# Attention with a GEGLU feed-forward on one Trainium2 core: more seven-product pairs in the last blocks, with their steps in turns

## The chip, the core and the metric

The kernel runs on one NeuronCore of a Trainium2 chip. Times are device microseconds of that core; the time of a kernel is the median of several executions, and one execution is profiled. Five engines work in parallel, each through its own queue in order: PE (TensorE, matrix products into PSUM), ACT (ScalarE), DVE (VectorE), POOL (GpSimd) and SP (SyncE, which issues most DMAs). An engine waits for another through semaphores. PEld is TensorE's weight load, which overlaps its products.

## The reference

```python
def _attn_ref(q, k, v):                       # q, k, v: (8, 8, 576, 64) float32
    q_s = np.exp(q - max over d);  q_s = q_s / sum over d
    k_s = np.exp(k - max over s);  k_s = k_s / sum over s
    kv = einsum('bhsd,bhse->bhde', k_s, v)
    return einsum('bhsd,bhde->bhse', q_s, kv)

def _moe_ref(x, w_gate, w_val, w_out):        # x: 4608 tokens x 512
    g = x @ w_gate                            # 512 x 1536
    gelu = 0.5 * g * (1 + erf(g / sqrt(2)))
    val = x @ w_val                           # 512 x 1536
    return (gelu * val) @ w_out               # 1536 x 512
```

The heads of the attention output are laid side by side (8 heads x 64 = 512 columns) and go into the feed-forward part as x. Nearly all arithmetic is in the three products with the weights.

## The kernel before, in words

**Blocks.** The 4608 tokens are worked on in nine blocks of 512. Blocks 0 to 7 are the batches, of whose 576 tokens 512 each; block 8 is made of the 64 remaining tokens of every batch (`xtr`). The order is 0 to 6, then 8, then 7 (`order`, L507). A block has a gate stage (g and val for 12 slices of 128 columns of the inner width, the result in `ht`) and an output stage. The program is written out in the order of its instructions for every engine; `at(block, kind, place, ...)` (L844) hangs attention work and other side work into places of that order and `ride` (L926) emits it. So what is written first stands first in its engine's queue.

**Gate stage, blocks 3 and later** (`fi_pairs`, L583). A slice can be computed classically (`half`, L587: four matmuls of 512 tokens for g, four for val; ACT takes the Gelu of g into a tile of the tag `gl`, DVE multiplies into `ht`). Or two slices, k and k + 3, make a *pair* and are computed with seven products on quarters (Strassen's scheme in Winograd's form): `product_gv` (L572), each of four matmuls of 256 tokens, 28 for the pair where the classical way has 16 of 512. Three pairs (k = 0, 1, 2: slices 0 to 5) are done so, slices 6 to 11 classically. For the pairs the kernel needs sums of the weights (`sum_wgv`, L556, on DVE into `ws`, one sum in place in the weights) and of x (`sum_x`, L566, four on POOL into `xs`, which has one buffer).

A pair in four steps of the queue, with `half` calls between them:
1. product 1 into bank pa, copied by ACT into pb (L623); product 5 into pc, snapshot s5 by ACT (`snap`, L606);
2. product 6 added in pa, snapshot s2; product 3 added in pc; DVE writes `cc[:, 0]` (`add`, L611); pc is free;
3. product 7 added in pa, DVE writes `cc[:, 1]`; product 2 added in pb, `final` (L599: ACT Gelu `glq`, DVE product into `ht`); then the upper half: ACT's Gelu `glc` of `cc` (L639) and POOL's product into `ht` (L640);
4. product 4 added in pa, which DVE must have read for `cc[:, 1]`; `final`.

`gl`, `glq`, `glc` and the output stage's snapshots `sn` share the tag `gl` with four buffers in turn; `cc` has one buffer. Banks of PSUM go round in a ring (`big`, L80); `hold` keeps one until `let_go`.

**Output stage** (`out_strassen`, L668): seven products again, of twelve matmuls each (`product`, L651), in the order 1 (psa), 2 (psb), 5 (psc), 6 (psa), 3 (psc), 7 (psa), 4 (psa). It needs sums of `ht` (`sum_h`, L542) for 5, 6, 3 and 7; sums 1 and 2 of a group are on DVE, sums 3 and 4 on DVE or POOL. The groups j = 0 and 1 come in the gate stage after their pair (kind PR, L923), the last group at the output stage's start (L961). DVE snapshots psa and psc (L690) before the next product is added into them. In block 8 `late` is set (L707): product 2 stands after product 7, and one of the sums moves.

**Side work.** Per batch: Exp of q and k on ACT, sums and reciprocals of q's rows on DVE (`norm_sum`, L210, one for each pair of heads; `norm_pair`, L219, for two of them), products with them on POOL (`norm_mul`), a transposing DMA (`unit_td`, L359), the cast of v on POOL (`cast_v`, L201, 640 columns at a time), the product of k and v (`unit_kv4`, L312) and of q with that into x (`unit_x4`, L398, at place NS 4, between products 7 and 4 of the block before). The 64 remaining rows of batch 0 go their own way: loaded by two DMAs into `q0r` with batch 2 (L851), `exp_rem0` (L240) at the end of block 2, `norm_rem0` (L244) on DVE and a transposing DMA (`unit_trem`, L350) in block 3, multiplied in block 3's NS 4 (L914). Tiles for q rows after Exp (`eq`, two buffers) and for loaded k (`kt`, two buffers) take turns by batch.

Of the kernel before, what the change touches and what calls it, by code (L numbers as in the profile page):

```python
# [18 lines left out]
def kernel(  # L19
# [86 lines left out]
    for i in range(2):  # L106
# [6 lines left out]
    ws = {nm: const.tile([P, 3, 2, NO // 2 * P], f16, name=f"ws{nm}") for nm in "gv"}  # L113
    xs = const.tile([P, 4, 2, 256], f16)
    q0r = const.tile([64, H, D], f32)
    eq0r = const.tile([P, C], f16)
    ld_b = {nm: [const.tile([P, H, NC * D], f32, name=f"{nm}t{i}") for i in range(n)]
            for nm, n in (("k", 2), ("v", 1), ("q", 1))}

# [29 lines left out]
    def load(src, nm, b, h0, h1, n0):  # L149
        tiles[(nm, b)] = ld_b[nm][b % len(ld_b[nm])]  # L150
        for t, c0 in ((0, n0), (1, 1)):
            (nc.scalar if b == 0 and t == 1 else nc.sync).dma_start(
                out=tiles[(nm, b)][t:P:2, h0:h1, c0 * D:NC * D],
                in_=src[b, h0:h1].rearrange("h (m n) d -> m h (n d)", n=NT)[
                    :, :, (4 * t + c0) * D:(4 * t + NC) * D])
# [36 lines left out]
    def exp(nm, b, h0=0, h1=H, n0=0):  # L192
        dst = ek_b[0] if nm == "k" else eq_b[b % 2]
        o, i = (("p n (c t d) -> p c t n d", "p c t (n d) -> p c t n d") if b >= QUAD else
                ("p n (h d) -> p h n d", "p h (n d) -> p h n d"))
        nc.scalar.activation(  # L196
            out=dst[:, n0:NC, h0 * D:h1 * D].rearrange(o, d=D, **({"t": 2} if b >= QUAD else {})),
            in_=heads(tiles[(nm, b)], b, h0, h1)[..., n0 * D:NC * D].rearrange(i, d=D),
            func=ACTF.Exp)
# [10 lines left out]
    def norm_sum(b, hp, n0=0):  # L210
        n = NC - n0
        e = eq_b[b % 2][:, n0:NC, hp * P:(hp + 1) * P].rearrange("p n (h d) -> p n h d", d=D)
# [6 lines left out]
    def norm_pair(b, g, n0, engs):  # L219

        n = NC - n0
        e = eq_b[b % 2][:, n0:NC, 2 * g * P:(2 * g + 2) * P].rearrange("p n (h d) -> p n h d", d=D)
# [16 lines left out]

    def exp_rem0():  # L240
        nc.scalar.activation(out=eq0r[0:64, :].rearrange("p (h d) -> p h d", d=D), in_=q0r,
                             func=ACTF.Exp)

    def norm_rem0():  # L244
# [5 lines left out]
        nc.vector.tensor_tensor(  # L250
# [84 lines left out]
    def unit_t(b, g, eng="dve", between=()):  # L335
# [3 lines left out]
        for j in range(2):  # L339
            hp = 2 * g + j  # L340
            for f in between if j == 1 else ():
                f()
            for n in range(NM):
                nc.tensor.transpose(
                    pst[:, j, n * P:(n + 1) * P],
                    eq_b[b % 2][:, n + 1, hp * P:(hp + 1) * P], ident)
# [3 lines left out]
    def unit_trem(b):  # L350

        src = eq0r[0:64] if b == 0 else eq_b[b % 2][:, 0, :]
# [6 lines left out]
    def unit_td(b):  # L359
# [3 lines left out]
                                    in_=eq_b[b % 2].rearrange("p n c -> p (n c)"))  # L363
# [192 lines left out]
    def sum_wgv(nm, i):  # L556
        w = wg_sb if nm == "g" else wv_sb
        n = NO // 2 * P
        a11, a21 = w[:, 0:2, 0:n], w[:, 0:2, n:2 * n]
        a12, a22 = w[:, 2:4, 0:n], w[:, 2:4, n:2 * n]  # L560
        t = [ws[nm][:, i] for i in range(3)]
# [10 lines left out]
    def product_gv(i, ps, xt, k, first):  # L572
        lo, hi = slice(k * P, (k + 1) * P), slice((k + NO // 2) * P, (k + NO // 2 + 1) * P)
        for t, w, nm in ((0, wv_sb, "v"), (1, wg_sb, "g")):
            for c in range(2):
                a = {1: w[:, c, lo], 2: w[:, 2 + c, lo], 3: ws[nm][:, 2, c, lo], 4: w[:, 2 + c, hi],
                     5: ws[nm][:, 0, c, lo], 6: ws[nm][:, 1, c, lo], 7: w[:, c, hi]}[i]
# [5 lines left out]
    def fi_pairs(b, xt):  # L583
        cs = [(c, nm) for k in range(NO // 2) for c in (NO + k, NO + NO // 2 + k) for nm in "gv"]
        psg = {}

        def half(n):  # L587
            c, nm = cs[n]
            t = big([P, 512], f32, "ps" + nm)
            mm_gv(t, wg_sb if nm == "g" else wv_sb, xt, c, range(HP))  # L590
            if nm == "g":
                psg[c] = ffn.tile([P, 512], f32, name="gl", tag="gl")
                nc.scalar.activation(out=psg[c], in_=t, func=ACTF.Gelu)  # L593
            else:
                nc.vector.scalar_tensor_tensor(out=ht[:, c, :], in0=t, scalar=_H_SCALE,  # L595
                                               in1=psg[c], op0=ALU.mult, op1=ALU.mult)
            ride(b, HF, n)

        def final(ps, fi):  # L599
# [6 lines left out]
        def snap(ps):  # L606
            sn = ffn.tile([P, 2, 256], f32, name="snq", tag="snq", bufs=3)
# [6 lines left out]

        ride(b, HF, -1)
        half(0)
        half(1)
        for k in range(NO // 2):
            cc = ffn.tile([P, 2, 2, 256], f32, name="cc", tag="cc", bufs=1)
# [6 lines left out]
            s5 = snap(pc)  # L626
            half(3 * k + 2)
# [5 lines left out]
            half(3 * k + 3)  # L633
# [4 lines left out]
            glc = ffn.tile([P, 2, 256], f32, name="glc", tag="gl")  # L638
            nc.scalar.activation(out=glc, in_=cc[:, :, 1], func=ACTF.Gelu, scale=1.0 / _H_SCALE)  # L639
            nc.gpsimd.tensor_tensor(  # L640
                out=ht[:, k:NO:NO // 2, 256:512], in0=cc[:, :, 0], in1=glc, op=ALU.mult)
            half(3 * k + 4)
            product_gv(4, pa, xt, k, False)
            final(pa, k + NO // 2)
            if k == NO // 2 - 1:
                half(11)
            ride(b, PR, k)
# [3 lines left out]
    def product(i, ps, first, ts=(0, 1)):  # L651
        for j in range(NO):
            for t in ts:
# [5 lines left out]
                if w is None:  # L659
# [3 lines left out]
                                 stop=(j == NO - 1), skip_group_check=True)  # L663

# [3 lines left out]
    def out_strassen(b, last):  # L668
# [38 lines left out]
        late = b == B  # L707
        get("a")
        product(1, ps["a"], True)
        s1 = snap("a")  # L710
        if not late:
            second()
# [5 lines left out]
        s5 = snap("c")  # L718
        if late:
            sum_h(*last_js(b), (3,))  # L720
# [4 lines left out]
        add("c", s2, 0, 1)  # L725
        for x in tiles_["c"]:
            let_go(x)
# [7 lines left out]
        ride(b, NS, 4)  # L735
        if late:
# [104 lines left out]
    FI, NS, HF, PR = range(4)  # L841
# [7 lines left out]
    def load_2nd():  # L849
        load_batch(2, ((q, "q"), (k, "k")))  # L850
        for h0 in (0, 4):  # L851
            nc.sync.dma_start(out=q0r[:, h0:h0 + 4], in_=q[0, h0:h0 + 4].rearrange(
                "h (m n) d -> m h (n d)", n=NT)[:, :, 0:D])
# [42 lines left out]
    at(2, FI, NFI - 1, L(exp, "q", 4), L(exp, "k", 4), exp_rem0)  # L896
    at(3, HF, 8, L(norm_rem0))
    at(3, HF, 11, L(unit_trem, 0))
    for b in range(3, B):
        n = b + 1  # L900
        if n < B:
            at(b, HF, -1, L(norm_sum, n, 0), L(norm_mul, n, 0, "pool"), L(norm_sum, n, 1),
               L(norm_mul, n, 1, "pool"))
            at(b, HF, 1, L(norm_sum, n, 2), L(norm_mul, n, 2, "pool"))
            at(b, HF, 2, L(norm_sum, n, 3), L(norm_mul, n, 3, "pool"))
            at(b, HF, 3, L(unit_td, n))
        if n + 1 < B:
            at(b, HF, 0, L(load_2, n + 1))
            at(b, HF, 5, L(cast_v, n + 1, 0, 4))
            at(b, HF, 8, L(cast_v, n + 1, 4, 8))  # L910
            at(b, HF, 11, L(exp, "q", n + 1), L(exp, "k", n + 1))
    for b in range(2, B - 1):
        n = b + 1
        at(b, NS, 4, L(unit_x4, n, ("act", "dve"), 0 if n == 4 else None))  # L914
# [4 lines left out]
        at(b, NS, 4, L(preload, ACTF.Gelu), L(lambda n: sum_x(get_xt(n)), n) if n < B - 1 else L(sum_x, xtr))  # L919
    at(B, NS, 2, L(lambda: sum_x(get_xt(B - 1))))  # L920
    for b in range(3, B + 1):
        for j in range(NO // 2 - 1):
            at(b, PR, j, L(sum_h, j, NO, (1, 2)), L(sum_h, j, NO, (3, 4), "pool"))  # L923
# [6 lines left out]
    for b in order:  # L930
# [9 lines left out]
        if b > 2:  # L940
            fi_pairs(b, xt)
# [51 lines left out]
```

## Time and profile before

| what | us |
|---|---|
| median of 3 runs | 301.37 (301.36 to 301.57) |
| the profiled execution | 301.16 |
| its span, first to last instruction | 299.4 |
| block 3, gate stage from 113.87 | 21.6 |
| blocks 4, 5, 6, gate stages from 146.28, 176.73, 206.91 | 19.5 to 19.6 each |
| output stages of blocks 4 and 5 | 10.9, 10.6 |
| block 8, gate stage from 236.55, output stage from 256.08 | 19.5, 10.35 |
| block 7, gate stage from 266.43; output stage from 285.96 to the end | 19.5, 13.4 |

The page gives the busy time of each engine. A block can be found in PE's timeline by its first `psg` matmul after the `psa<-tw,ht` ones of the output stage. A matmul's own duration (0.27 us at 256 tokens, 0.38 at 512) is longer than the distance to the next one, since matmuls are pipelined; ACT and DVE instructions overlap their followers by about 0.1 us too. A timeline's columns are start, duration, engine, line, operation, output from inputs, shapes and count, and in brackets the idle time before and what ended it. The table of stretches gives, for a window, its length and each engine's busy time and instructions.

### The profile page before, as it was taken

To read this page: it belongs to the slowest core of one execution; us is meant where nothing else is said; L and a number is where in the kernel's file an instruction comes from. 1 tells how busy PE (TensorE), PEld (TensorE's weight loads), DVE (VectorE), ACT (ScalarE), POOL (GpSimd) and SP (SyncE) were. 2 spreads that over 40 slices of the span, in tenths; PEclk is the share of its full clock that TensorE was granted. 3 is DMA by queue.
4 is the path that set the end of the run, shared out by engine and by line. 5 is a ranking of instruction groups with operands and counts; after the bars stand their busy time and mean duration, and the time that the engine had idled before them with its cause. 6 is when DMAs were issued, how large, how long until landed. Compare 5 with 4: busy or idle time off the path is not lost. (4 is left out here: it accounts for less than half of the span.)

```text
span 299.4 us, 5905 instructions
## 1 busy us (share of the span) xinstructions
PE 287.1 (96%) x2293; PEld 188.4 (63%) x2293; DVE 213.5 (71%) x411; ACT 173.1 (58%) x269; POOL 161.7 (54%) x149
## 2 busy tenths in 40 slices
PE   3999999999999999899999999999999999899994
PEld 1544445446744586568666876687668666676683
DVE  2953479998767889786867786878687557845762
ACT  4763467777652576558656956595652465126530
POOL 1557558870336009991599359944981536803610
PEclk9999999999999999999999999999999999999999
DMA  7999999997189106960399029802140300023003
GB/s 225 372 383 390 400 389 388 332 319 208 74 286 306 42 2 227 384 100 2 127 344 233 3 113 347 242 2 101 54 77 0 123 21 0 2 61 81 0 2 140
DMA packets 54619, 51.69 MB, mean 173 GB/s; under 512 B 18496, under 2 KB 50496, under 8 KB 54592
## 3 DMA queue, kind: packets, MB, share of 16 engines
q1 hardware_dynamic: 52864, 49.49, 52.0%
q10 hardware_dynamic: 1728, 1.84, 1.9%
q8 instruction: 18, 0.29, 0.4%
q14 instruction: 9, 0.07, 0.1%
HBM read 37.75 MB, written 9.44 MB: 158 GB/s over the span
## 5 line engine op out<-in xcount | busy, mean ns | idle before, releaser
L443 PE MATMUL psg<-xt,wg_sb 128*128 128x512 f16 x264 | 69.8, 379 | 0.0
L443 PE MATMUL psv<-xt,wv_sb 128*128 128x512 f16 x264 | 69.7, 379 | 0.0
L443 PEld LDWEIGHTS <-wv_sb 128*128 128x128 f16 x288 | 28.1, 98 | 27.4 <-issue 0.2
L233 POOL TENSOR_TENSOR eq<-eq,rrq 128x640 f16<-128x640 f16 (+1 forms) x27 | 34.5, 1297 | 19.7 <-DVE rrq L226 7.3
L443 PEld LDWEIGHTS <-wg_sb 128*128 128x128 f16 x288 | 28.1, 98 | 25.3
L661 PEld LDWEIGHTS <-ht 128*128 128x128 f16 x384 | 37.2, 98 | 7.1 <-issue 0.8
L448 ACT ACTIVATE gl<-psg 128x512 f32<-128x512 f32 x36 | 21.0, 597 | 29.0 <-PE psg L443 28.9
L640 POOL TENSOR_TENSOR ht<-cc,glc 128x512 f16<-128x512 f32 x18 | 22.8, 1267 | 24.1 <-ACT glc L639 24.1
L449 DVE SCALAR_TENSOR_TENSOR ht<-psv,gl 128x512 f16<-128x512 f32 x36 | 24.2, 684 | 16.0 <-PE psv L443 13.7
L570 POOL TENSOR_TENSOR xs<-xt 128x512 f16<-128x512 f16 x10 | 12.0, 1200 | 43.1 <-ACT xt L174 43.1
L595 DVE SCALAR_TENSOR_TENSOR ht<-psv,gl 128x512 f16<-128x512 f32 x36 | 24.6, 684 | 4.5 <-PE psv L443 2.4
L593 ACT ACTIVATE gl<-psg 128x512 f32<-128x512 f32 x36 | 21.3, 591 | 7.9 <-PE psg L443 7.8
L172 POOL CAST v<-vt 128x640 f16<-128x640 f32 x26 | 19.1, 769 | 12.0 <-PE pskv L319 10.5
L661 PE MATMUL psa<-tw,ht 128*128 128x256 f16 x192 | 23.5, 273 | 0.2 <-DVE yo L696 0.2
L214 DVE TENSOR_REDUCE rq<-eq 128x10 f32<-128x640 f16 x28 | 22.2, 793 | 1.6 <-ACT eq L196 1.6
L196 ACT ACTIVATE ek<-kt 128x1280 f16<-128x1280 f32 (+1 forms) x11 | 19.1, 1748 | 5.6 <-DMA kt<-in_k_dram 4.1
L580 PEld LDWEIGHTS <-wv_sb 128*128 128x128 f16 x144 | 14.0, 98 | 12.8 <-DVE cc L612 1.8
L661 PEld LDWEIGHTS <-sh 128*128 128x128 f16 x192 | 18.7, 98 | 3.5 <-issue 1.0
L552 POOL TENSOR_TENSOR ht<-ht 128x512 f16<-128x512 f16 x12 | 16.7, 1396 | 6.5 <-DVE sh L552 6.5
L196 ACT ACTIVATE eq<-qt 128x2560 f16<-128x2560 f32 (+2 forms) x10 | 18.4, 1863 | 2.6 <-DMA qt<-in_q_dram 2.5
L601 ACT ACTIVATE glq<-pgb 128x256 f32<-128x256 f32 x18 | 6.9, 383 | 21.6 <-PE pgb L580 21.2
L612 DVE SCALAR_TENSOR_TENSOR cc<-pgc,snq 128x512 f32<-128x512 f32 x18 | 12.4, 686 | 7.5 <-ACT snq L608 7.5
(136 smaller groups left out, 566.5 us busy)
## 6 DMA issues: line engine op xcount, KB each, us to landing
out_dram<-yo SPq DMA_DIRECT2D x15, 512.0 KB, 3.4
kt<-in_k_dram SPq DMA_DIRECT2D x7, 640.0 KB, 8.4
vt<-in_v_dram SPq DMA_DIRECT2D x7, 640.0 KB, 5.1
qt<-in_q_dram SPq DMA_DIRECT2D x7, 640.0 KB, 6.8
qt<-in_q_dram SPq DMA_DIRECT2D x8, 512.0 KB, 7.4
wost<-in_moe_w_out_dram SPq DMA_DIRECT2D x6, 512.0 KB, 7.9
kt<-in_k_dram SPq DMA_DIRECT2D x6, 512.0 KB, 9.8
vt<-in_v_dram SPq DMA_DIRECT2D x6, 512.0 KB, 5.7
```

The source lines that it names most:

```text
L172: nc.gpsimd.tensor_copy(out=dst, in_=src)
L196: nc.scalar.activation(out=dst[:, n0:NC, h0 * D:h1 * D].rearrange(o, d=D, **({"t": 2} if b >= QUAD else {})), in_=heads(tiles[(nm, b)], b, ...
L214: nc.vector.reduce_sum(rq, e, axis=mybir.AxisListType.X)
L233: (nc.gpsimd if eng == "pool" else nc.vector).tensor_tensor(out=e, in0=e, in1=rrq.unsqueeze(-1).to_broadcast((P, n, 2, D)), op=ALU.mult)
L443: nc.tensor.matmul(ps, w[:, ci, fi * P:(fi + 1) * P], xt[:, ci, :], start=(ci == 0), stop=(ci == HP - 1))
L448: nc.scalar.activation(out=gl, in_=psg, func=ACTF.Gelu)
L449: nc.vector.scalar_tensor_tensor(out=ht[:, fi, :], in0=psv, scalar=_H_SCALE, in1=gl, op0=ALU.mult, op1=ALU.mult)
L552: (nc.gpsimd if eng == "pool" else nc.vector).tensor_tensor(out=o, in0=a, in1=b, op=op)
L593: nc.scalar.activation(out=psg[c], in_=t, func=ACTF.Gelu)
L595: nc.vector.scalar_tensor_tensor(out=ht[:, c, :], in0=t, scalar=_H_SCALE, in1=psg[c], op0=ALU.mult, op1=ALU.mult)
L640: nc.gpsimd.tensor_tensor(out=ht[:, k:NO:NO // 2, 256:512], in0=cc[:, :, 0], in1=glc, op=ALU.mult)
L661: nc.tensor.matmul(ps[t], a, w, start=(first and j == 0 and (t == ts[0] or ps[t].tensor is not ps[ts[0]].tensor)), stop=(j == NO - 1), ski ...
```

## The change

It touches the gate stages of blocks 3 to 8.

- **Pairs.** Blocks 4, 5 and 6 compute a fourth pair (k = 6: slices 6 and 9) with seven products, blocks 8 and 7 all six pairs (k = 0, 1, 2, 6, 7, 8) and no slice classically. Block 3 keeps three.
- **Order.** A string per block lists the steps: `k.i` is step i of pair k, `7g` and `7v` are the halves of a classical slice, letters are places for side work, `s0` and `s1` the sums of `ht`. In blocks 8 and 7, and in part of 4 to 6, the steps of two pairs take turns. The last step of the last pair (8.4) stands in the output stage after product 1, its upper half goes to DVE and is written after step 2.4, and the first step of block 7 stands in block 8's output stage before product 4.
- **Weight sums** for the new pairs are made on DVE at the places NS 1, 2 and 3 of the output stages of blocks 3 to 6, in the space of the second `kt` buffer. `cc` gets a second buffer in the space of the second `eq` buffer. So from batch 4 on k and q have one buffer each. `snq` has four buffers, not three.
- **Norm sums** from block 3 on are taken by two head pairs at once (`norm_pair`), both products on POOL.
- **Batch 0's remainder** is loaded in block 4, in two tiles, its Exp is at the end of block 4, its norm in block 5 (NS 2, product on POOL), its transposing DMA in block 6, its product in block 6's NS 4.
- Block 8's output stage has the common order (`late = False`). The preload of the Gelu table is left out in block 6's NS 4. Small sums of x: in block 6 for block 8.

```diff
+    def buf(bs, b):
+        return bs[b % len(bs) if b < 4 else 0]
...
-    def sum_wgv(nm, i):
+    def sum_wgv(nm, i, k=0, n=NO // 2):
...
-        nc.vector.tensor_tensor(
+        nc.gpsimd.tensor_tensor(
             out=e, in0=e, in1=rrq.unsqueeze(-1).to_broadcast((64, H, D)), op=ALU.mult)
...
+    THREE = ("a 6g l 6v n 0.1 9g 0.2 9v t 0.3 7g 0.4 s0 1.1 7v c 1.2 10g 1.3 10v 1.4 s1 2.1 8g d 2.2"
+             " 8v 2.3 11g 2.4 11v e")
+    FOUR = ("a 7g l 7v n 0.1 10g 0.2 10v t 0.3 6.1 0.4 8g 6.2 8v c 6.3 1.1 6.4 s0 2.1 1.2 2.2 d 1.3"
+            " 2.3 11g 1.4 s1 2.4 11v e")
+    SIX = ("0.1 6.1 0.2 6.2 0.3 6.3 0.4 1.1 6.4 s0 7.1 1.2 7.2 1.3 7.3 1.4 2.1 7.4 s1 8.1 2.2 8.2"
+           " 2.3 8.3 2.4")
+    steps = {b: (THREE if b == 3 else SIX if b >= B - 1 else FOUR).split() for b in range(3, B + 1)}
...
+        def upper(cc):
+            glc = ffn.tile([P, 2, 256], f32, name="glc", tag="gl")
+            nc.scalar.activation(out=glc, in_=cc[:, :, 1], func=ACTF.Gelu, scale=1.0 / _H_SCALE)
+            (nc.vector if k == NFI - NO // 2 - 1 else nc.gpsimd).tensor_tensor(
+                out=ht[:, k:k + NO // 2 + 1:NO // 2, 256:512], in0=cc[:, :, 0], in1=glc, op=ALU.mult)
+
+        if i == 1:
+            live["odd"] = odd = not live.get("odd", True)
+            cc = cc_b if odd else ffn.tile([P, 2, 2, 256], f32, name="cc", tag="cc", bufs=1)
...
+            if k == NFI - NO // 2 - 1:
+                live["upper"] = lambda: upper(cc)
+            else:
+                upper(cc)
...
-        late = b == B
+        late = False
         get("a")
         product(1, ps["a"], True)
         s1 = snap("a")
+        if b >= B - 1:
+            pair_step(b, get_x(b), NFI - NO // 2 - 1, 4)
         if not late:
             second()
...
         s5 = snap("c")
+        ride(b, NS, 1)
...
         add("c", s2, 0, 1)
+        ride(b, NS, 3)
...
         ride(b, NS, 4)
+        if b == B:
+            go_on(B - 1, get_x(B - 1), 1)
...
+            at(b, PR, "a", L(norm_pair, n, 0, 0, ("pool", "pool")))
+            at(b, PR, "n", L(norm_pair, n, 1, 0, ("pool", "pool")))
+            at(b, PR, "t", L(unit_td, n))
         if n + 1 < B:
+            at(b, PR, "l", L(load_2, n + 1))
+            at(b, PR, "c", L(cast_v, n + 1, 0, 4))
+            at(b, PR, "d", L(cast_v, n + 1, 4, 8))
+            at(b, PR, "e", L(exp, "q", n + 1), L(exp, "k", n + 1))
+    at(4, PR, "l", load_rem0)
+    at(4, PR, "e", exp_rem0)
+    at(5, NS, 2, norm_rem0)
+    at(6, PR, "t", L(unit_trem, 0))
...
     for b in range(3, B + 1):
         for j in range(NO // 2 - 1):
-            at(b, PR, j, L(sum_h, j, NO, (1, 2)), L(sum_h, j, NO, (3, 4), "pool"))
+            at(b, PR, f"s{j}", L(sum_h, j, NO, (1, 2)), L(sum_h, j, NO, (3, 4), "pool"))
+    for b, i, what in ((3, 1, "g1 v1"), (3, 2, "g2 v2 g3 v3"), (3, 3, "g4 v4")):
+        for x in what.split():
+            at(b, NS, i, L(sum_wgv, x[0], int(x[1]), NO, 1))
+    for b, i, what in ((4, 1, "g1"), (4, 2, "g2 g4"), (4, 3, "v1"), (5, 1, "v2"), (5, 3, "v4"),
+                       (6, 1, "g3"), (6, 2, "v3")):
+        for x in what.split():
+            at(b, NS, i, L(sum_wgv, x[0], int(x[1]), NO + 1, 2))
```

## The prediction

> **What bounds the kernel now.** I read part 1 of the page first, then the table of stretches, cut at the first matmul of each block's gate stage, then PE's waits, and last the timelines of the engines around those waits.
>
> ```profile
> PE 287.1 (96%) x2293; PEld 188.4 (63%) x2293; DVE 213.5 (71%) x411; ACT 173.1 (58%) x269; POOL 161.7 (54%) x149
> ...
> core 0: us, PE busy (x) PEld busy (x) DVE busy (x) ACT busy (x) POOL busy (x), PEclk, DMA share, GB/s
> 146.28:165.85 19.57, 19.57 (x135) 12.90 (x132) 14.37 (x30) 13.01 (x27) 18.41 (x18) 1.00 0.86 242
> 206.91:226.44 19.53, 19.53 (x135) 12.92 (x132) 14.57 (x30) 12.94 (x27) 16.68 (x15) 1.00 0.25 61
> 236.55:256.08 19.53, 19.53 (x134) 12.91 (x132) 11.07 (x22) 12.55 (x25) 11.45 (x10) 1.00 0.07 29
> ...
> PE pga L580 <- DVE cc L612: 1.8, 2, 1.4
> PE psa L661 <- DVE sn L690: 0.8, 1, 0.8
> ```
>
> TensorE is never idle in the gate stages of blocks 4 (first stretch), 6 and 8, at granted clock 1.00, so a column less is time less. But POOL is busy for 18.41 us of block 4's 19.57; the average of 54% hides that. PE's waits are few: two in block 3 (product 4 waits for `cc`) and one in block 8's output stage.
>
> ```profile
> 256.50 1.15 POOL L570 TENSOR_TENSOR xs<-xt 128x512 f16<-128x512 f16 x1
> 257.73 1.22 POOL L570 TENSOR_TENSOR xs<-xt,xs 128x512 f16<-128x512 f16 x1
> 258.91 1.33 POOL L570 TENSOR_TENSOR xs<-xt 128x512 f16<-128x512 f16 x1
> ...
> 257.11 0.82 DVE L552 TENSOR_TENSOR sh<-ht 128x512 f16<-128x512 f16 x1
> 257.97 1.26 DVE L552 TENSOR_TENSOR sh<-sh,ht 128x512 f16<-128x512 f16 x1
> 259.15 0.68 DVE L690 TENSOR_SCALAR sn<-psa 128x512 f32<-128x512 f32 x1
> ...
> 259.88 1.47 PE L661 MATMUL psa<-tw,sh 128*128 128x256 f16 x12 [0.84 <-DVE sn L690]
> ```
>
> This is block 8's end; the last line is product 6. The DVE sums `sh` take 0.42 us alone; here 0.82 and 1.26, and each ends 0.28 us after the POOL instruction during which it began (257.65 and 258.95). The same holds at 65.66 (0.82) and 93.52 (0.84 where 0.55 is usual) beside a POOL cast. So **a DVE sum of two SBUF tensors waits for the running POOL instruction**; evacuations from PSUM (0.68) don't.
>
> **Gains.** Matmuls start 0.2163 us apart at 512 columns and 0.1092 at 256 (starts in the timeline of block 8). A classical pair is 16 x 0.2163 = 3.46; a seven-product pair 28 x 0.1092 = 3.06; 0.403 less. Nine pairs change (one each in blocks 4, 5, 6, three each in 8 and 7): **-3.63**. The weight loads, 98 ns each, still fit under 109. Block 8's wait above cost 1.17 with the gap inside the product before; the new order of that stage removes it: **-1.17**. Block 3: product 4 is 1.52 late at 122.33 behind four norm sums (115.76 to 120.42, 4.08 without the evacuation between), and 0.58 at 134.21 behind `norm_rem0` (1.57 of DVE). The reduce takes 0.793 at 640 elements and 1.216 at 1024, so 1.50 at 1280 (between 1.22 and 1.59); with reciprocals two pairs take 3.42, so 0.61 less, and the second wait goes: **-1.19**. Block 4's 0.24 at 171.32 goes with its new order. Sum **-6.2**.
>
> **Losses in blocks 4 to 6.** I lay the new order out from the block's first matmul (0), with starts back to back as the timelines of block 8 show: ACT 0.49 to 0.50 for 512, 0.27 for 256, 0.54 for `glc`; DVE 0.61, 0.34, and sums 0.46 + 0.35; POOL product 1.27, sums 1.39 + 1.15, cast 0.69; hand-over about 0.05. The four pairs and eight halves take PE 19.15. POOL ends the norm products at 8.6 as before (154.92 - 146.28), then: product of pair 0 to 9.8, casts "c" to 11.2, product of pair 6 from 12.3 to 13.6 (its `glc` waits for step 6.3). At s0 DVE's sums wait for the final of 6.4: P4 ends at 12.3, ACT first has the copy and snapshot of 1.1, so the Gelu starts at 13.15 and DVE is done at 14.0. POOL's two sums then run to 17.1, casts "d" to 18.4, products of pairs 1 and 2 to 19.7 and 20.9. POOL has 18.41 + 1.27 = 19.7 us of work for 19.15: it is the engine that becomes late.
>
> Who waits: the tag `gl` has four buffers; step 1.4's Gelu gets the one that `glc` of pair 1 holds until POOL's product at 19.7. So its final ends at 20.5. Behind it on DVE stand the sums of s1, the first of which begins during POOL's product of pair 2 and ends 0.28 after it, 21.2; the second 21.6; only then comes the final of step 2.4, at 22.0. Output product 1 reads that row (ht 5) with its last two matmuls, due 1.09 after its start at 19.15 + 0.27 (0.27 are short waits in the steps, by the same laying): 20.5. **1.5 late.** Next: POOL's s1 sums run 21.3 to 23.8; DVE's last sums begin at 22.6, are held to 24.1 and 24.5; the snapshot ends at 25.1, the one of psc at 27.15. Products 5, 6 and 3 wait 0.1, 0.2 and 0.7: **1.0**. Blocks 4 and 5: 0.27 + 2.54 each. Block 6 has no casts: 0.27 + 0.83 + 1.02. Sum **+7.7**.
>
> **Losses in blocks 8 and 7.** Per pair ACT needs 3 x 0.495 + 0.54 + 2 x 0.27 = 2.57, DVE 2 x 0.61 + 2 x 0.345 + 0.4 = 2.3, POOL 2.5, all under PE's 3.06; but the order in the queues costs: copy of pair 7 stands behind the Gelu of 6.4, and `cc` of 1.3 behind it in turn: 0.16 + 0.06 + 0.06 + 0.18 per two pairs, twice: 0.95 a block. In the end stage, from the start of product 1: the final of 2.4 is done at 1.28, which costs 0.24; POOL's product of pair 2 ends at 1.53; DVE's `upper` of pair 8 runs 1.3 to 2.0 (a row bounds it: 0.42 to 0.69, taken 0.69); the last sums begin at 2.05. In block 8 POOL runs `sum_x` from 1.5: the sums are held to 3.0 and 4.3, the snapshot ends at 4.9, and only then the final of 8.4, at 5.25. Product 2 needs its row at 3.08: **2.2 late**. In block 7 POOL is idle: final at 3.6, 0.59 late. Sum 2 x 0.95 + 2 x 0.24 + 2.2 + 0.6 + 0.1 = **+5.3**.
>
> [...]
>
> **Edits costed at nothing, with their cover.** The weight sums at NS 1 to 3 are DVE work of 1.9 (block 3: eight of 256 columns), 1.5, 0.7 and 0.7 us; 512 columns take 0.42 (`sh`), 256 I take as 0.29 by the step 0.42 to 0.55 of 512 to 768, bounds 0.2 and 0.42. They lie behind snapshots where DVE idles (0.53, 0.62, 0.62 in block 5's output stage; 8.37 busy of 10.88 in block 4's). Without that cover up to 4.8. `norm_rem0` in block 5: 0.9 of DVE in the same idle time; its POOL product (1.48 for a like one of 128 rows) when POOL is idle. Two small DMAs of q go from batch 2's loads to behind batch 6's on SP's queue, before a transposing DMA that waited for POOL until 185.20 anyway (loads issued by 183.6); the transposing DMA of the remainder goes to block 6, used 12 us later. `exp_rem0` as two instructions: 0.76 of ACT before a wait of 2.5. One k and one eq buffer from batch 4 on: loads of k issue 6 us after the Exp that frees them, Exp of q starts 4.7 after the transposing DMA landed.
>
> **Sum.** -6.2 + 7.7 + 5.3 = **+6.7** (rounded). The profiled execution took 301.16 (span 299.4 and 1.8 around it), 0.2 under the median of 301.37: 301.2 + 6.7 = **307.9**. Laid in the same way, the old order ends within 0.2 us of the profile, so the forecast rests on the new order's waits.
>
> **Rivals.** (1) *TensorE stays the bound, faster.* The output-stage losses (5.1 + 1.85 + 2.5 + 0.8 = 10.2) all hang on DVE standing in front of finals and snapshots for POOL's last product. If that lands some 2.3 us earlier than I say (by 18.6 in blocks 4 to 6), they go, and 297.7 results. For: PE never idles in the old stages, DVE and ACT have a third to spare. Against: 18.41 of 19.57 on POOL, and one product added. (2) *Slower by less.* The hold of DVE by POOL applies only beside `sum_x`-like pairs or is rarer than laid: the queue order remains (about 1.4 in each of blocks 4 and 5, 0.7 in 6, 1.1 and 0.6 in the last two, 0.27 to 0.95 inside). These sum to 7.9 and give 302.9. For: in blocks 4 to 7 now every sum takes 0.42. Against: there they never meet POOL; where they do (four places) they are held. (3) *The waits cancel the gain:* POOL about 1.5 us earlier in blocks 4 to 6 alone takes 7 us off: 300.9.
>
> **Chances.** Forecast (304.5 to 310.7) 0.62; rival 2 (302 to 304.5) 0.18; above 310.7, as when the weight sums lose half their cover and the step waits double, 0.03; no change 0.05 (within 0.2%, 0.6 us, about what a measurement can tell); rival 1 0.12. Faster 0.12, same 0.05, slower 0.83. The range reaches from 302.0 to 310.7 and leaves out 0.2.
>
> **What would show it.** Right: PE waits in product 1 of blocks 4 and 5 for `ht` from DVE (L602 of before), about 1.5 each; psc waiting for a snapshot by 0.7; `sh` sums above 0.8 us in blocks 4 to 6 and 8; POOL's product of pair 2 ending over 1 us into the output stage; product 2 of block 8 late by 2. Wrong: POOL done before the output stage, or sums of 0.42 beside POOL work. PE busy should fall by some 3.6.

## The result and the profile after

The changed kernel takes **309.82 us** in the median of four executions (308.1, 309.65, 310.0, 310.04), the kernel before 301.42 (301.36 to 301.57): a ratio of 1.027, with a 95% interval of 1.023 to 1.030. The forecast was 307.9 in a range of 302.0 to 310.7. The profiled execution of the changed kernel took 310.0, its span is 308.1.

The first part of the page after the change, and the table of stretches for the gate stages of blocks 4 and 6 (columns as in the prediction's table; each window ends some 0.1 before its stage does):

```profile
PE 290.5 (94%) x2401; PEld 198.8 (65%) x2401; DVE 225.8 (73%) x430; ACT 186.2 (60%) x305; POOL 171.5 (56%) x157
...
core 0: us, PE busy (x) PEld busy (x) DVE busy (x) ACT busy (x) POOL busy (x), PEclk, DMA share, GB/s
145.12:164.50 19.38, 19.32 (x146) 14.07 (x144) 13.51 (x24) 13.62 (x29) 17.14 (x17) 1.00 0.87 252
210.09:229.40 19.31, 19.27 (x146) 14.04 (x144) 13.69 (x24) 13.85 (x30) 14.99 (x14) 1.00 0.27 66
```

PE is nowhere really idle inside the gate stages, and they are hardly shorter than before: by the starts in PE's timeline blocks 4 to 6 take 19.46 to 19.49 (19.53 to 19.57 before), block 8 takes 19.01 (19.53). What the page gives as busy rose by 3.4 us although the pairs save PE work. Part of that is a stretch at half clock, shown below; part are short waits, which lie within the modelled ends of the matmuls and count as busy. So the share in part 1 tells little here; the waits tell more. PE's waits after the change, without the first row (4.9 us at the kernel's start, as before) and the last (0.3, for `kv_sb`):

```profile
PE psb L706 <- DVE ht L629: 3.0, 2, 2.4
PE psa L706 <- DVE ht L629: 2.7, 3, 1.0
PE psc L706 <- DVE sn L738: 1.7, 3, 0.6
PE pga L601 <- DVE cc L639: 0.6, 1, 0.6
```

All four name DVE, none POOL. The first is product 2 of blocks 8 and 7, the second product 1 of blocks 4 to 6, the third product 3 of the same blocks, which waits for the snapshot of psc; the last is product 4 of block 3. The length of a block, from its first gate matmul to the next block's, shows where the time went (starts in PE's timelines; "side work alone" is the run e4 below, which has none of the new pairs):

| kernel | block 3 | 4 | 5 | 6 | block 8's start to PE's last matmul |
|---|---|---|---|---|---|
| before | 32.41 | 30.45 | 30.18 | 29.64 | 58.76 |
| after | 30.97 | 32.50 | 32.47 | 31.41 | 62.85 |
| side work alone | 30.96 | 30.18 | 30.18 | 29.64 | 58.76 |

Block 3 gained 1.44, blocks 4 to 6 lost 6.1, blocks 8 and 7 lost 4.1.

**Blocks 4 to 6.** The end of block 4's gate stage: timelines of POOL, DVE and PE.

```profile
163.39 1.28 POOL L645 TENSOR_TENSOR ht<-eq,glc 128x512 f16<-128x512 f32 x1
164.62 1.28 POOL L645 TENSOR_TENSOR ht<-cc,glc 128x512 f16<-128x512 f32 x1
...
165.46 0.71 DVE L572 TENSOR_TENSOR sh<-ht 128x512 f16<-128x512 f16 x1
166.21 0.42 DVE L572 TENSOR_TENSOR sh<-sh,ht 128x512 f16<-128x512 f16 x1
166.55 0.42 DVE L629 SCALAR_TENSOR_TENSOR ht<-pga,glq 128x256 f16<-128x256 f32 x1
...
167.03 0.39 PE L706 MATMUL psa<-wo_sb,ht 128*128 128x256 f16 x2 [1.03 <-DVE ht L629]
```

POOL's products for the upper halves of pairs 1 and 2 end at 164.67 and 165.90, the second some 1.3 us after the gate stage is over on PE. DVE's first sum of s1 is held by this second product (0.71 in place of 0.42) and ends 0.27 after it; the second sum follows; only then comes the final of step 2.4, for which the last two matmuls of product 1 wait.

That POOL's last product lands so late is not new. The same place before the change, one row each of POOL, DVE and PE:

```profile
166.08 1.27 POOL L640 TENSOR_TENSOR ht<-cc,glc 128x512 f16<-128x512 f32 x1
167.38 0.43 DVE L552 TENSOR_TENSOR sh<-ht 128x512 f16<-128x512 f16 x1 [0.44 <-POOL ht L640]
165.85 1.47 PE L661 MATMUL psa<-wo_sb,ht 128*128 128x256 f16 x12
```

It ended 1.50 after the gate stage (21.07 after the block's start, now 20.77), and product 1 ran through, since the finals stood ahead of the sums that waited for it. What did move is POOL's product before it, pair 1's: it ended 15.47 after the block's start and ends 19.55 now. For this one step 1.4's Gelu waits (for the buffer, as predicted), and behind its final come the sums of s1, which stand ahead of the final of 2.4.

**Block 8.** Its output stage on POOL (the sums of x), DVE and PE:

```profile
262.06 1.60 POOL L589 TENSOR_TENSOR xs<-xt 128x512 f16<-128x512 f16 x1
263.74 1.21 POOL L589 TENSOR_TENSOR xs<-xt,xs 128x512 f16<-128x512 f16 x1
264.91 1.33 POOL L589 TENSOR_TENSOR xs<-xt 128x512 f16<-128x512 f16 x1
...
261.84 0.81 DVE L645 TENSOR_TENSOR ht<-cc,glc 128x512 f16<-128x512 f32 x1
262.75 1.19 DVE L572 TENSOR_TENSOR sh<-ht 128x512 f16<-128x512 f16 x1
263.98 1.25 DVE L572 TENSOR_TENSOR sh<-sh,ht 128x512 f16<-128x512 f16 x1
265.15 0.68 DVE L738 TENSOR_SCALAR sn<-psa 128x512 f32<-128x512 f32 x1
265.75 0.41 DVE L629 SCALAR_TENSOR_TENSOR ht<-pga,glq 128x256 f16<-128x256 f32 x1
...
266.22 0.39 PE L706 MATMUL psb<-wo_sb,ht 128*128 128x256 f16 x2 [2.44 <-DVE ht L629]
266.45 2.40 PE L706 MATMUL psc<-tw,sh 128*128 128x256 f16 x12
```

DVE's two sums take 1.19 and 1.25, each ending 0.27 to 0.28 after a sum on POOL; the snapshot and the final stand behind them, and PE is idle for 2.44. By the distance of the starts, product 2 is 2.60 late (the idle time in brackets is shorter, since it counts from the modelled end of the matmul before).

The last line has something that was in no forecast: the twelve matmuls of product 5 take 2.40, where twelve take 1.47 elsewhere. The stretches behind the wait, with the granted clock in the third column from the end:

```profile
266.20:268.00 1.80, 1.78 (x11) 1.37 (x12) 1.35 (x3) 0.00 (x0) 1.16 (x2) 0.67 0.00 0
268.00:270.50 2.50, 2.50 (x14) 1.86 (x13) 0.70 (x2) 0.00 (x0) 0.00 (x0) 0.55 0.00 0
270.50:273.00 2.50, 2.50 (x25) 2.24 (x24) 1.38 (x2) 0.00 (x0) 0.00 (x0) 1.00 0.03 7
```

From 266.82 to 270.24 the granted clock is 0.5, and matmuls of 256 columns start 0.213 apart, not 0.109. Half the speed for 3.42 us costs 1.71. The execution of 308.1 us had a mean clock of 0.999, the three others 0.993 to 0.994: this is the difference between them.

### The profile page after: what moved, and what is told of

It is laid out like the page before. It is cut to its first block, busy times and chain, and to the rows that moved or that the text cites. A ratio compares the mean times of both kernels' runs of the same rounds, so it can differ in the third digit from the quotient of the medians.

```text
span 308.1 us, 6204 instructions
## 1 busy us (share of the span) xinstructions
PE 290.5 (94%) x2401; PEld 198.8 (65%) x2401; DVE 225.8 (73%) x430; ACT 186.2 (60%) x305; POOL 171.5 (56%) x157
## 5 line engine op out<-in xcount | busy, mean ns | idle before, releaser
L463 PE MATMUL psg<-xt,wg_sb 128*128 128x512 f16 x216 | 57.4, 379 | 0.0
L463 PE MATMUL psv<-xt,wv_sb 128*128 128x512 f16 x216 | 57.4, 379 | 0.0
L706 PEld LDWEIGHTS <-ht 128*128 128x128 f16 x384 | 36.5, 98 | 14.8 <-DVE ht L629 8.3
L468 ACT ACTIVATE gl<-psg 128x512 f32<-128x512 f32 x36 | 21.0, 598 | 29.0 <-PE psg L463 28.9
L469 DVE SCALAR_TENSOR_TENSOR ht<-psv,gl 128x512 f16<-128x512 f32 x36 | 24.2, 684 | 16.0 <-PE psv L463 13.7
L463 PEld LDWEIGHTS <-wg_sb 128*128 128x128 f16 x216 | 21.0, 98 | 20.7
L645 POOL TENSOR_TENSOR ht<-eq,glc 128x512 f16<-128x512 f32 x13 | 16.6, 1275 | 19.6 <-ACT glc L644 19.6
L629 DVE SCALAR_TENSOR_TENSOR ht<-pga,glq 128x256 f16<-128x256 f32 x27 | 11.4, 422 | 21.3 <-ACT glq L628 21.3
L601 PEld LDWEIGHTS <-wv_sb 128*128 128x128 f16 x216 | 20.9, 98 | 8.6 <-DVE cc L639 1.1
L654 ACT COPY pgb<-pga 128x512 f32<-128x512 f32 x27 | 15.8, 587 | 13.6 <-PE pga L601 13.6
L706 PE MATMUL psa<-tw,ht 128*128 128x256 f16 x192 | 23.5, 273 | 0.1
L601 PEld LDWEIGHTS <-wg_sb 128*128 128x128 f16 x216 | 21.1, 98 | 2.5
L706 PEld LDWEIGHTS <-sh 128*128 128x128 f16 x192 | 19.4, 102 | 4.1 <-DVE sh L572 0.7
L601 PE MATMUL pga<-xs,wv_sb 128*128 128x256 f16 x108 | 20.6, 272 | 0.7 <-DVE cc L639 0.6
L601 PE MATMUL pga<-xs,wg_sb 128*128 128x256 f16 x108 | 20.6, 272 | 0.0
```

What stands on the lines that cost most here:

```text
L463: nc.tensor.matmul(ps, w[:, ci, fi * P:(fi + 1) * P], xt[:, ci, :], start=(ci == 0), stop=(ci == HP - 1))
L468: nc.scalar.activation(out=gl, in_=psg, func=ACTF.Gelu)
L469: nc.vector.scalar_tensor_tensor(out=ht[:, fi, :], in0=psv, scalar=_H_SCALE, in1=gl, op0=ALU.mult, op1=ALU.mult)
L601: nc.tensor.matmul(ps[:, t], a, x, start=(first and t == 0 and c == 0), stop=(c == 1), skip_group_check=True)
L645: (nc.vector if k == NFI - NO // 2 - 1 else nc.gpsimd).tensor_tensor(out=ht[:, k:k + NO // 2 + 1:NO // 2, 256:512], in0=cc[:, :, 0], in1=g ...
L654: nc.scalar.copy(out=pb, in_=pa)
```

## The experiments

Theory A is the prediction's: the loss is DVE, on which sums of `ht` that wait for POOL stand ahead of finals and snapshots. Theory B: the steps of two pairs in turns lose time in the hand-overs between PE, ACT and DVE, or POOL simply has too much work. Theory C is of the clock. The times of the kernel before beside these runs were 301.41, 301.26 and 301.28.

**e4: the side work alone.** No new pairs and no new sums of weights; norm sums by two head pairs, batch 0's remainder in block 5, block 8 and 7 as before.

```diff
-    steps = {b: (THREE if b == 3 else SIX if b >= B - 1 else FOUR).split() for b in range(3, B + 1)}
+    steps = {b: THREE.split() for b in range(3, B + 1)}
...
-        late = False
+        late = b == B
...
```

> No new pair and no new weight sums: only norm sums by two head pairs and batch 0's remainder moved, with the order as before otherwise. Theory A: block 3's product 4 is late by 0.8 once, not by 1.5 and 0.6: 299.9 (1.4 under before). If the norm sums are hidden anyway: 301.4.

Measured: **299.43** (299.06 to 299.6), ratio 0.9925 (0.990 to 0.995). Block 3 is 1.45 shorter and block 4 0.27, the rest is as before. This part of the change is a gain of 2.0; the pairs lose some 10 in the changed kernel.

**e1 and e2: the fourth pair alone, and the six pairs alone** (each with the side work and the sums of weights that it needs; in e1 the output stages of blocks 8 and 7 have the order that e4 gives them).

```diff
# e1: FOUR in blocks 4 to 6, blocks 8 and 7 as before
+    steps = {b: (FOUR if 3 < b < B - 1 else THREE).split() for b in range(3, B + 1)}
...
# e2: SIX in blocks 8 and 7, blocks 4 to 6 as before
+    steps = {b: (SIX if b >= B - 1 else THREE).split() for b in range(3, B + 1)}
...
```

> Blocks 4 to 6 in the new order with the fourth pair; blocks 8 and 7 with three pairs and the output order of before. Theory A (DVE stands in front of finals and snapshots for POOL's last products in blocks 4 to 6; and, apart from that, for sum_x in block 8): the losses of blocks 4 to 6 stay whole, those of 8 and 7 go: 306.3, about 5 over before, product 1 of blocks 4 and 5 late by 1.2 to 1.4. Theory B (the cost is in the hand-overs of two pairs in turns, so in the blocks with six pairs): 299 to 300, under before. Theory C (the loss is TensorE's lower clock alone): within 1 us of before less the columns, 299.

> Blocks 4 to 6 with three pairs, 8 and 7 with six. Theory A: 303 to 303.8: the columns of six pairs (2.4) and block 3's 1.2 are gained, block 8's 2.6 and the slow clock behind it (1.7), block 7's 0.75 and the short waits in the steps (0.9 a block) are lost. Theory B: 308 or more, since the turns are all here. Theory C: as A.

Measured: e1 **305.61** (305.56 to 305.64), ratio 1.0128 (1.009 to 1.017); e2 **301.73**, ratio 1.0028 (1.000 to 1.005). Against e4, the fourth pair costs 6.2 and the six pairs 2.3 without the clock. Together 8.5 + 299.43 = 307.9, beside 308.1 for the execution of the changed kernel at full clock: the two parts add up. In e1 blocks 4 to 6 take 32.47, 32.44 and 31.40, as in the changed kernel, and nothing after them differs from before.

The ten executions of e2 fall into two groups: six at 301.63 to 301.74 with a mean clock of 0.999 to 1.0, four at 303.33 to 303.52 with 0.993 to 0.994. The profiled execution is that of 301.63: product 2 is 2.60 late in it, as in the changed kernel, and the clock stays at 1.00 behind it. The 303 to 303.8 expected for e2 holds for the four alone; the median is 1.3 lower.

**e3: the sums of x tied behind DVE's sums.** POOL's sums of x in block 8 have to wait for a one-element write on DVE that stands behind the last sums of `ht`.

```diff
-    at(B, NS, 2, L(lambda: sum_x(get_x(B - 1))))
+    at(B, NS, 2, L(nc.vector.memset, xs[:, 0, 0, 0:1], 0.0), L(lambda: sum_x(get_x(B - 1))))
```

> The changed kernel, with block 8's four sums of x on POOL held back until the output stage's snapshots are done (one DVE write of one element into their first output). Theory A: DVE's last two sums take 0.42 each, product 2 is late by 0.6 to 0.9 instead of 2.6, TensorE's clock doesn't drop, 306 to 306.7. If POOL doesn't hold DVE here: no change, 309.8. If the clock drops for another reason: 308.2.

Measured: **306.40** (306.31 to 306.59), ratio 1.0155 (1.010 to 1.021), clock 0.998 to 1.0 in all four. DVE's and PE's timelines at the same place:

```profile
262.60 0.42 DVE L572 TENSOR_TENSOR sh<-ht 128x512 f16<-128x512 f16 x1
263.06 0.42 DVE L572 TENSOR_TENSOR sh<-sh,ht 128x512 f16<-128x512 f16 x1
263.40 0.68 DVE L738 TENSOR_SCALAR sn<-psa 128x512 f32<-128x512 f32 x1
264.00 0.41 DVE L629 SCALAR_TENSOR_TENSOR ht<-pga,glq 128x256 f16<-128x256 f32 x1
...
264.47 0.39 PE L706 MATMUL psb<-wo_sb,ht 128*128 128x256 f16 x2 [0.84 <-DVE ht L629]
```

Without POOL beside them the same two sums take 0.42 each, and product 2 is 1.00 late in place of 2.60. So 1.6 of the 2.60 were the hold, and the last 1.0 is the order on DVE itself. The low clock went with it: of the 3.4 us to the changed kernel's median 1.6 are the hold, and 1.7 what lies between its executions at 308.1 and at 309.8.

**e6: the sums of s1 behind step 2.4** in blocks 4 to 6.

```diff
-            " 2.3 11g 1.4 s1 2.4 11v e")
+            " 2.3 11g 1.4 2.4 s1 11v e")
```

> The changed kernel, with the last place of sums (s1) written behind step 2.4 in blocks 4 to 6 in place of before it. Theory A (the final of 2.4 is late only because DVE's two sums, held by POOL's product, stand in front of it): the wait of 1.20 in product 1 of blocks 4 and 5 and of 0.81 in block 6 shrinks to under 0.4; but the two sums and all that follows on DVE end later by about as much, so that the waits of psc and of products 5, 6 and 3 grow from about 1.0 to some 1.9 a block; in all about 0.3 a block less: 308.9 where the clock drops after block 8's wait, 307.2 where it does not. Theory B (the final is late because its Gelu's buffer comes free late, whatever stands on DVE): product 1 waits 1.2 as before, 309.8 (308.1 without the drop).

Measured: 307.05, 307.18 and 307.45 at clock 0.998 to 1.0, and 308.78 at 0.994; median 307.31, ratio 1.0211 (1.019 to 1.023). PE's timeline in block 4:

```profile
164.60 1.71 PE L706 MATMUL psa<-wo_sb,ht 128*128 128x256 f16 x12
166.15 1.56 PE L706 MATMUL psb<-wo_sb,ht 128*128 128x256 f16 x12
167.54 1.52 PE L706 MATMUL psc<-tw,sh 128*128 128x256 f16 x12
169.91 1.47 PE L706 MATMUL psa<-tw,sh 128*128 128x256 f16 x12 [0.85 <-DVE sn L738]
```

Product 1 now runs nearly through (1.71 against 1.47), so the buffer of the Gelu wasn't what held the final: theory A. But product 6 now waits 1.01 (0.17 in the changed kernel) for the snapshot behind the delayed sums; a block gains 0.26, about the 0.3 expected. Moving an instruction in DVE's queue moves the wait; the work before POOL's last product has to end earlier.

**e7: no casts of v.** The casts of v of batches 5, 6 and 7 on POOL are left out of blocks 3 to 5.

```diff
-            at(b, PR, "c", L(cast_v, n + 1, 0, 4))
-            at(b, PR, "d", L(cast_v, n + 1, 4, 8))
```

> The changed kernel without the two casts of v on POOL in blocks 3, 4 and 5: v of batches 5, 6 and 7 is not converted, which leaves out 2.6 us of POOL's work in each of these gate stages. Theory A (POOL has more work than the stage is long, and DVE's sums wait for its last products): in blocks 4 and 5 the wait in product 1 falls from 1.20 to about 0.8, as block 6 has it, which has no casts; about 1.4 less in all: 308.4 with the clock drop, 306.7 without. It does not vanish, since POOL's products still wait for the Gelus of the pairs in turns. Theory B (POOL's load has no part in it, the order of the queues on DVE and ACT alone sets the waits): 309.8 (308.1 without the drop), product 1 late 1.20.

Measured: 307.62 at clock 0.998, and 309.01 to 309.15 at 0.993 to 0.994 (three executions). Product 1 is 0.82 and 0.81 late in blocks 4 and 5, the number of block 6. Blocks 4 and 5 are 0.52 shorter each, 1.05 in all where 1.4 was expected. POOL's load has its part, but two thirds of the wait stay with 2.6 us of work fewer: most of it is the order, not the amount.

**e8 and e9: the order mended.** e8 has three pairs in blocks 4 to 6 and six in blocks 8 and 7, where the final of 8.4 is written ahead of the snapshot and of DVE's last sums, with the tie of e3. e9 has the fourth pair as well, in another order of its steps.

```diff
     # output stage, both
         product(1, ps["a"], True)
-        s1 = snap("a")
         if b >= B - 1:
             pair_step(b, get_x(b), NFI - NO // 2 - 1, 4)
+        s1 = snap("a")
+        if b >= B - 1:
+            sum_h(*last_js(b), (1, 2))
...
-    at(B, NS, 2, L(lambda: sum_x(get_x(B - 1))))
+    at(B, NS, 2, L(nc.vector.memset, xs[:, 0, 0, 0:1], 0.0), L(lambda: sum_x(get_x(B - 1))))
...
     # e9 alone
-    FOUR = ("a 7g l 7v n 0.1 10g 0.2 10v t 0.3 6.1 0.4 8g 6.2 8v c 6.3 1.1 6.4 s0 2.1 1.2 2.2 d 1.3"
-            " 2.3 11g 1.4 s1 2.4 11v e")
+    FOUR = ("a n 0.1 6.1 0.2 l 7g 6.2 0.3 7v t 6.3 10g 6.4 c 0.4 10v 1.1 s0 2.1 1.2 2.2 1.3 8g 2.3 8v"
+            " 1.4 2.4 s1 11g 11v d e")
```

> Three pairs in blocks 4 to 6 as before, six pairs in blocks 8 and 7 as changed; in their output stages the final of step 8.4 is written ahead of the snapshot and the last sums of ht on DVE, and the sums of x in block 8 wait for a one-element write on DVE behind those sums. The norm parts of the change are in. Theory A (product 2's 2.60 is nothing but DVE's queue held by POOL): product 2 late by under 0.4 in both blocks, no clock drop, 299.2, that is 2.2 under the kernel before. Theory B (the six pairs cost in the hand-overs between PE, ACT and DVE inside the gate stage, and the wait only moves to products 5 and 3): at least 301, as the version with six pairs alone has it (301.7).

> As the one above, and with the fourth pair in blocks 4 to 6, its steps in another order: pair 6 follows pair 0 at once, the casts and the products of the classical slices come after it, the last sums stand behind the final of 2.4, and two classical slices come last. Theory A (the fourth pair's 6.2 us are all waits for DVE and POOL at the end of the gate stage, so an order that ends POOL's products early keeps the 1.2 that the three pairs save on PE): no wait above 0.3 in the output stages of blocks 4 to 6, 298.0, which is 3.4 under the kernel before. Theory B (POOL is short of time whatever the order: 19.7 us of work in a stage of 19.2): the wait comes back at another place, 300 or more.

Measured: e8 **299.00** (298.93 to 299.07), ratio 0.9925 (0.991 to 0.994); e9 **298.43** (298.41 to 298.74), ratio 0.9909 (0.990 to 0.992): 2.8 us faster than the kernel before and the fastest of all. In e8 product 2 is 0.07 late in both blocks. e9's timelines at the end of block 4 (POOL, DVE, PE):

```profile
161.88 1.27 POOL L645 TENSOR_TENSOR ht<-cc,glc 128x512 f16<-128x512 f32 x1
...
162.61 0.80 DVE L629 SCALAR_TENSOR_TENSOR ht<-pga,glq 128x256 f16<-128x256 f32 x2 [0.22 <-ACT glq L628]
163.32 0.42 DVE L572 TENSOR_TENSOR sh<-ht 128x512 f16<-128x512 f16 x1
163.77 0.43 DVE L572 TENSOR_TENSOR sh<-sh,ht 128x512 f16<-128x512 f16 x1
...
164.09 1.47 PE L706 MATMUL psa<-wo_sb,ht 128*128 128x256 f16 x12
165.40 1.47 PE L706 MATMUL psb<-wo_sb,ht 128*128 128x256 f16 x12
```

POOL's last product ends at 163.15, before the sums begin, and holds none of them; the sums take 0.42, the finals stand before them, and products 1 and 2 run through. e9 changes both POOL's times and the order on DVE, so it doesn't say what each is worth. Theory B's POOL that is too full falls: in this stage POOL is busy for 17.40 us of 18.94 and no wait of PE comes of it there. But theory B isn't empty. The fourth pair gains 0.57 over e8, not 1.2, since product 3 still waits 0.25 a block for psc's snapshot, behind a DVE sum that POOL holds (1.26). And in e8 the steps in turns cost 0.95 and 0.90 inside the gate stages of blocks 8 and 7, which no order of the output stage touches. Another 1.3 are short waits: 0.22 at block 8's start, 0.26 in product 1 of each block, 0.27 and 0.13 in block 8's products 5 and 3, and 0.07 three times. That is why six pairs, which save 6 x 0.403 = 2.4 on PE and remove block 8's old wait of 1.17, bring only 0.4 over e4.

**e10 and e11: the clock.** e10 puts 20 matmuls whose result is never read into PE's wait in block 8; e11 lengthens that wait by writing DVE's second sum twice.

```diff
     # e10, in product 2 of block 8, ahead of its last two matmuls
+                for _ in range(20):
+                    nc.tensor.matmul(fill, ht[:, 0, 0:P], wo_sb[:, 0, 0:256], start=True, stop=True,
+                                     skip_group_check=True)
...
     # e11
-            sum_h(*last_js(b), (1, 2))
+            sum_h(*last_js(b), (1, 2, 2) if b == B else (1, 2))
```

> The changed kernel, with 20 extra matmuls of 128x256 in block 8's product 2, ahead of the two that wait for the last row of ht; their result goes into the bank of product 5, which starts afresh, so that it is never read. At 0.109 us each they take 2.2 of the 2.44 us in which PE is idle, and the last two matmuls are as late as before. Theory C (the clock drops because PE is idle for 2.44 us): no drop in any execution, clock 0.998 to 1.0 in all, 308.1 to 308.3 in each. Rival (the drop has another cause, such as the load on the chip at this point or earlier in the kernel): part of the executions at 309.7 to 310.0 with clock 0.993, as the changed kernel and the version with six pairs alone have.

> The changed kernel, with the second of block 8's last two sums of ht written twice on DVE (the same values once more). Each of the sums there waits for one of POOL's sums of x (1.21 to 1.33 us), so the final of 8.4 and the end of PE's wait come some 1.2 to 1.3 us later: PE idle for 3.7 us where it was 2.44. Theory C (an idle time that fills, or nearly fills, a window of the clock's control lowers the clock): the drop in nearly all executions, clock 0.993 or less, 309.8 + 1.3 = 311.1, perhaps up to 1.7 more where the low clock lasts twice as long; none at 309.4. Rival (the drop comes by chance and does not depend on the length of the idle time): about half of the executions at 309.4 and half at 311.1. If DVE's third sum is not held, 0.42 more in place of 1.3.

Measured: e10 **308.01** (307.8 to 308.31, five executions, clock 0.997 to 1.0), ratio 1.0222 (1.021 to 1.024). e11, six executions with their mean clocks: 309.29 (0.998), 309.44 (0.998), 310.72 (0.994), 310.83 (0.993), 312.17 (0.989), 312.22 (0.989). PE's timelines, e10 first (the extra lines shift L706 to L710 in it; L700 are the added matmuls):

```profile
262.61 1.25 PE L710 MATMUL psb<-wo_sb,ht 128*128 128x256 f16 x10
263.70 2.35 PE L700 MATMUL psc<-wo_sb,ht 128*128 128x256 f16 x20
266.31 0.39 PE L710 MATMUL psb<-wo_sb,ht 128*128 128x256 f16 x2 [0.26 <-DVE ht L629]
266.54 1.47 PE L710 MATMUL psc<-tw,sh 128*128 128x256 f16 x12
```

```profile
267.30 0.39 PE L706 MATMUL psb<-wo_sb,ht 128*128 128x256 f16 x2 [3.72 <-DVE ht L629]
267.53 1.47 PE L706 MATMUL psc<-tw,sh 128*128 128x256 f16 x12
```

In e10 the last two matmuls are as late as in the changed kernel, PE is busy meanwhile, and no execution loses the 1.7: the idle time is the cause. The rival of e10 falls, as far as five executions say it: if each had an even chance of the drop, all five would be spared once in 32 times. In e11 there are three times: no drop, one drop (+1.4) and a drop of twice the cost (+2.8). The last was foreseen as possible only, and the first against expectation: in the profiled execution, of 309.29, PE is idle for 3.72 and the product behind it takes 1.47, at full clock. The chance of a drop is higher than with 2.44 (4 of 6 against 11 of 22), but a longer wait doesn't make it sure; the last section has what the drops go with.

## Why the prediction came out as it did

The time lay in the range, and the waits came where the prediction had laid them and about as long: DVE stands in front of finals and snapshots. The forecast of 307.9 is what the changed kernel takes when the clock holds (308.1, and 308.0 in e10). The clock was in no term; that the median still lies in the range is the breadth of the range, which reached 2.8 above the forecast. Term by term, without the clock unless said; measured terms are differences of the block lengths to those of e4, the PE work saved added:

| term | predicted | measured |
|---|---|---|
| nine pairs on PE | -3.63 | matmuls start 0.109 apart as taken |
| block 3 | -1.19 | -1.44 |
| block 4's old wait | -0.24 | -0.27 |
| block 8's old wait | -1.17 | not there any more |
| waits in blocks 4 to 6 | +7.7 | 2.32 + 2.29 + 1.77 + 3 x 0.403 = +7.6 |
| waits in blocks 8 and 7 | +5.3 | 61.15 (e10) - 58.76 + 2.42 + 1.17 = +6.0 |
| clock | none | +1.7 |
| sum | +6.7 | +8.8 (with -3.63 and -1.17 as predicted), and 310.0 - 301.16 = 8.8 |

- **Blocks 4 to 6.** Product 1 was foreseen 1.5 late in blocks 4 and 5 and is 1.32 (1.20 and 0.12); block 6 0.83 and is 0.81; products 5, 6 and 3 foreseen 0.1, 0.2, 0.7 and are 0.10, 0.17, 0.74. POOL's last product was foreseen 20.9 after the block's start and ends at 20.77; but it ended at 21.07 in the kernel before too, so "the engine that becomes late" is true of pair 1's product alone. e6 showed that the final is late because of what stands before it on DVE, e7 that the casts have the part that block 6 lacks.
- **Blocks 8 and 7.** The steps in turns cost 0.90 a block (0.95 foreseen), product 2 of block 7 0.74 (0.59). **Mis-sized** was "product 2 late 2.2 in block 8": it is 2.60. The prediction had POOL's sums of x follow each other 1.3 apart from 1.5 on; POOL's first sum of x, which began during DVE's `upper`, took 1.60 (1.15 to 1.33 at this place before); that moved the chain by 0.3. Another 0.22, between products 1 and 5 of block 8's first step, was not foreseen: product 5 reads POOL's first sum of x, which ends at 242.11, and starts at 242.16; before, classical slices came first there. The last 0.1 of that sum has no row in the prediction, and no run shows it as a wait; what comes near it is 0.07 between block 7's first step and product 4, and the 0.12 by which `upper` took longer than laid. e3 confirmed the step itself: without the hold 1.0 is left.
- **The clock** is the step that was missing. The prediction took PE's matmuls behind a wait at 0.109, as everywhere in the trace before, whose longest wait in the last blocks is 1.0. Behind 2.44 of idle time this doesn't hold in half of the executions (three of the changed kernel's four, which set its median; which of the executions drop is chance).
- **Block 3.** The reduce of 1280 elements takes 1.476 (1.50 taken); product 4 is 0.78 late where about 0.9 was left. (The prediction's own 4.08 less 3.42 is 0.66; it took 0.61.)
- **Edits costed at nothing** cost nothing: blocks 4 to 6 are as long in e2, which has all the weight sums, as in e4, which has none (30.18, 30.18, 29.64), and blocks 5 and 6 as long as before, with the remainder's norm in them.
- **The rivals.** That TensorE stays the bound (297.7) failed on the order alone: in e9 POOL's last product of block 4 ends 18.2 us after the block's start, where the prediction had asked for 18.6, the finals stand ahead of the sums, and e9 takes 298.4. The early landing alone isn't the condition: without the fourth pair (e4) POOL ends 20.0 to 20.9 after the starts of blocks 4 to 6, and no product 1 waits. "Slower by less", in which the hold is rare, failed: in blocks 4 to 6 and 8 every `sh` sum that began during a POOL instruction ended 0.28 after it (the longest took 1.38). Those that began first were not held (0.42 at 159.54, POOL's from 159.59).
- **A sign that failed.** PE busy was to fall by some 3.6 and rose by 3.4; even in e9, with the same nine pairs and none of the long waits, it falls only 1.4, to 285.7. So this share is no measure of the columns saved.
- **The product `upper` in f32.** It took 0.80 or 0.81 in every trace that has it, each time beginning during POOL's product and ending 0.55 after it; 0.69 was taken. Whether POOL's product costs the 0.12 isn't shown: no row has `upper` without POOL beside it.

## What to carry to other kernels

Work that an engine does for later (sums for product 5) must not stand ahead of what the next matmul reads, above all if it can be held by another engine, as the sums on DVE were by POOL (up to 1.38 in place of 0.42): look, for each wait, at what stands before the named instruction in its queue. A helper's last result may land after the stage ends, as it did before the change, if nothing that the next matmul reads stands behind it. Putting the same work into another order made 9.7 us here (e9 against the changed kernel's execution at full clock, 308.1 - 298.4). A long wait of TensorE can cost more than its length (1.3 to 1.9 us more in half of the executions with 2.44): keep it short, or fill it with matmuls that nobody reads (e10: no drop in five executions).

## What the runs showed of the hardware

After 2.44 us without a matmul the granted clock fell to 0.5 in 11 of 22 executions (the changed kernel 3 of 4, e2 4 of 10, e6 1 of 4, e7 3 of 4), for 3.41 us in the one whose profile shows it, at a cost of 1.3 to 1.9. After 3.72 us it fell in 4 of 6, in two of them at twice the cost. In the 29 executions of kernels whose waits in the last blocks are 1.0 or shorter, or filled (e1, e3, e4, e8, e9, e10), the mean clock was never under 0.997.

The traces show what the drops go with. In all twelve the granted clock changes only on a grid of 3.413 us, which lies differently in each: the stretches at full clock are 84 to 87 times that long (85 in the kernel before, 290.13 us), in the changed kernel 75 and 11 times (256.00 and 37.55 us), and the low one between them once. What the next step was granted goes with how much of one step of this grid PE was idle:

| idle time | share of a step | the next step |
|---|---|---|
| e3, e8, e9: behind the last matmul, to the end of that step | 0.47, 0.46, 0.55 | full clock |
| e2, e6, e7: wait of 2.44, cut by a border of the grid | 0.38, 0.59, 0.58 at most | full clock |
| e11: wait of 3.72, cut by a border | 0.53 and 0.56 | full clock |
| the changed kernel: wait of 2.44 within one step (263.41 to 266.82) | 0.71 | half clock |
| e10, e6, e7, e11: behind the last matmul | 0.69, 0.73, 0.74, 0.76 | half clock |
| all others: behind the last matmul | 0.95 to 1.00 | half clock |

The largest share with full clock behind it is 0.59, the smallest with half clock 0.69. An estimate from these rows: the limit lies between the two, at 2.0 to 2.4 us, and a wait drops the clock or not by where the grid falls on it. Estimated from that, if the grid falls anywhere with equal chance: a wait of 2.44 drops the clock in 0.34 to 0.54 of the executions, one of 3.72 in 0.71 to 0.91; seen were 11 of 22 and 4 of 6. Why two of e11's executions lost twice as much, no profile shows.
